# Retention and an MLP on one core: two tiles' 64-row matmuls in one visit, and another order of loads

## The chip, the core and the metric

The kernel runs on one core of a Trainium2 chip. The core has five engines that run side by side, each through its own list of instructions in order: TensorE (PE, matrix products, with its weight loads shown as PEld), VectorE (DVE), ScalarE (ACT), GpSimd (POOL) and SyncE (SP). They wait for one another by semaphores. Data comes by DMA, which an engine issues and which sixteen DMA engines carry out. The metric is the device time of one execution in microseconds (us), as the median of several.

## The reference, cut to what matters

There are 4 batches of 768 positions, 8 heads of 64. First comes a recurrence over positions, then a normalization and a two-layer perceptron with a residual.

```python
gamma = 1.0 - 2.0 ** (-5.0 - np.arange(H))
for t in range(S):
    state = gamma * state + einsum('bhd,bhe->bhde', k[:, :, t], v[:, :, t])
    y[:, :, t] = (1 / sqrt(D)) * einsum('bhd,bhde->bhe', q[:, :, t], state)
x = y.transpose(0, 2, 1, 3).reshape(B, S, 512)
xn = (x - mean(x)) / sqrt(var(x) + 1e-6) * g_ln
out = x + maximum(xn @ w_ch1, 0) @ w_ch2        # 512 x 2048, 2048 x 512
```

## The kernel before

The 768 positions of a batch are cut into 6 chunks of 128. A chunk of one batch is a tile, so there are 24 tiles of 128 rows by 512 columns. Tiles 0 to 3 are the first chunks of the four batches; tiles 4 to 8 are the other chunks of batch 0, tiles 9 to 13 those of batch 1, and so on.

Inside a tile the recurrence becomes matrix products. The tile's keys and queries are needed transposed. For tiles 0 to 7 PE transposes them (L498, L505) and ACT and DVE bring them from PSUM to SBUF, the queries times the decay `qsc` (L510, `eq`). For later tiles SP issues a transposing DMA (L520, `tr`) and DVE multiplies (L527). Then PE makes the scores of the 8 heads (`e_pa`, L538): 8 matmuls whose contraction is 64 rows, a head's width. DVE multiplies them by the decay mask (`e_am`, L562, `am`). The part of the result that comes from earlier chunks is queries times the state: for tiles 0 to 7 in full 128-row matmuls (L582), for tiles from 8 on (`T0`) in 8 matmuls of 64 rows (`e_ps`, L548), which stand right before the scores in most tiles. PE then adds masked scores times values (`e_py`, L572 and L586). The state is built by POOL (`vg`, L633: values times a decay), PE (`e_pd`, L645) and DVE (`e_pb`, L659).

DVE takes the tile's statistics (L601, L602, `bn`), then normalizes (L613, `xn`); ACT keeps a copy for the residual (L619, `xc`). From tile 8 on the result lies in two PSUM banks, even heads in one and odd heads in the other, so these steps work by halves. The normalized tile is transposed by PE (L672, tiles 0 to 7) or by a DMA (L686). The first layer (`e_m1`, L719) works on groups of 1, 2 or 4 tiles (8 groups of one, 4 of two, 2 of four), 16 matmuls of 128 columns, 16 of 256 in two pieces, or 4 of 512 to a piece; ACT, or DVE at L734, applies the relu (L732) into `h1`. The second layer (`e_m2`, L757) takes 16 matmuls of 512 columns to a tile, in four parts; DVE adds the residual (L767) and ACT issues the store (L774). Short idle times early on are filled with matmuls on zeros (L785, `warm`).

PSUM has eight banks: one for the state, two for the first layer, two for the scores, and three (`b0`, `b1`, `b2`) for the rest. Of these the late tiles' result holds `b1` and `b2`, and the second layer goes through `b0`, in the last tiles through all three.

The order of all instructions is fixed by hand: `ORDER` lists the numbers of the tasks in the order in which they are emitted, and each engine gets its own in that order. POOL issues all loads of q, k, v (L430; float32 in HBM, bfloat16 in SBUF) and of the weights in quarters (L438): v0, k1, q1, v1, the first quarter of w1, k2, q2, the second quarter, v2, k3, q3, v3, the third, and so on. The k and q of tile 0 come in halves through SP and ACT (L401). From tile 8 on, one-element copies (L447) hold POOL back until an earlier load has landed.

Of the kernel before, what the change touches and what calls it, by code (L numbers as in the profile page):

```python
# [14 lines left out]
PE, ACT, DVE, POOL, SP = range(5)  # L15

CFG = {
    "T0": 8, "TX": 8, "groups": [1] * 8 + [2] * 4 + [4] * 2,
    "first": ["iota", "pos", "v0", "k1", "q1", "v1", "w1_0", "k2", "q2", "w1_1", "v2",
              "k3", "q3", "v3", "w1_2", "k4", "q4", "v4", "k5", "q5", "v5", "w1_3", "w2_0",  # L20
              "k6", "q6", "v6", "k7", "q7", "v7", "w2_1", "w2_2", "w2_3"],
    "bufs": {"qsb": 6, "ksb": 5, "vsb": 9, "qk": 8, "tr": 6, "vg": 3, "trq": 3, "trk": 3},
    "load_pad": 600, "w_pad": 550, "lead": 32, "lead2": 32, "sq_at": 28000, "late_load": 1700, "two": 4, "m2b": ("b0",), "m2all": 16, "inter": 4, "every": 4, "tail": (0, 384, 512), "step": 8, "pace": 8, "ahead": 3,
    "slack": 600, "tr_pad": 4000, "x_pad": 3500, "vg_pad": 2500, "fill": 0.8, "fill_end": 14000,
}

ORDER = [int(x) for x in """
16 17 2 0 3 19 20 23 14 8 15 1 24 5 7 9 25 4 10 6 13 21 11 26 18 45 22 27 146 28 149  # L30
100147 148 150 46 29 151 30 162 100163 153 12 152 165 154 164 166 155 31 156 157 167 32
158 168 169 47 100176 159 170 524 177 178 160 179 100172 214 180 181 171 173 532 33 215
182 183 525 184 534 161 190 533 193 34 35 36 526 100191 186 535 192 194 10527 187 540 37
38 185 542 195 48 196 49 39 541 216 197 204 40 42 43 41 536 198 50 217 543 207 234
100205 206 528 537 200 52 51 201 544 199 208 10529 224 209 545 552 188 548 10549 553 174
100225 210 227 550 551 546 53 55 175 226 228 211 54 212 44 218 219 547 213 554 530 220
555 251 202 221 235 100241 229 538 230 56 244 10531 236 556 539 242 275 231 558 100258
557 232 559 243 560 10561 237 562 57 245 246 233 238 239 563 222 566 259 564 247 260 567
248 189 261 570 262 252 565 568 249 60 254 255 250 569 223 253 203 263 100722 61 268 58
59 62 287 298 63 723 716 724 301 66 67 64 717 65 264 725 269 718 571 719 265 726 266 270  # L40
720 576 100271 276 307 267 578 272 579 577 728 273 68 69 278 277 72 729 730 731 318 73
279 70 299 71 280 580 572 732 281 300 282 74 322 284 286 734 735 75 288 581 283 285 736
302 303 290 289 573 737 291 738 574 319 584 292 740 741 293 320 294 296 742 308 304 240
585 78 575 743 582 744 295 297 310 333 79 76 309 77 339 586 305 583 311 80 746 587 334
747 312 335 313 314 274 316 323 81 315 748 84 350 749 351 588 592 317 325 85 82 83 379
750 589 256 257 324 354 326 727 602 86 752 87 753 327 328 329 603 593 590 754 755 594
591 330 90 331 340 352 332 342 756 341 343 721 380 598 321 599 595 91 758 336 759 344
760 761 596 733 88 345 89 355 762 346 368 348 353 600 92 757 745 739 337 597 347 93 764
96 349 97 94 381 601 95 765 98 338 357 604 356 766 606 386 99 605 382 607 767 358 306
359 383 614 612 768 360 384 615 361 613 363 770 397 102 771 103 100 362 772 398 365 364  # L50
763 369 101 104 371 370 773 403 610 372 608 774 611 373 776 616 609 399 366 105 374 387
108 109 617 375 618 414 367 377 106 107 777 620 418 751 376 378 389 619 110 388 778 390
779 622 415 391 385 404 780 392 393 621 623 630 782 395 111 114 429 115 631 394 112 400
456 113 433 626 116 624 117 396 406 120 121 416 405 430 783 627 625 407 784 431 408 628
419 409 634 785 410 629 632 411 412 457 118 119 122 413 421 635 786 445 633 420 123 788
126 458 422 127 789 646 124 423 424 790 425 427 647 401 125 426 428 791 642 638 434 436
792 435 794 795 796 639 643 465 769 437 438 640 417 439 440 442 128 797 459 641 129 441
446 443 476 132 644 798 432 402 133 645 636 130 448 447 648 131 134 138 637 460 650 449
450 649 800 651 461 451 452 801 802 477 454 803 444 775 480 462 453 466 478 455 135 491
804 136 137 468 492 467 806 139 495 807 469 470 140 493 808 471 141 809 472 142 474 473  # L60
475 652 653 654 481 483 482 484 810 655 656 658 143 510 479 485 144 787 506 805 657 799
145 659 660 661 486 662 507 496 487 489 664 663 488 508 490 666 498 497 665 499 667 668
670 669 500 671 501 502 672 673 504 511 812 674 503 505 676 513 512 675 514 678 463 677
680 515 679 682 813 681 814 683 516 494 811 509 517 781 519 464 518 520 815 100830 831
816 521 832 818 819 200824 820 825 684 817 793 685 826 690 688 691 827 689 694 696 833
695 522 686 697 687 708 709 821 698 699 692 693 523 822 848 700 828 834 702 100842 701
703 706 707 704 200836 714 837 705 715 712 838 849 843 713 710 711 850 844 845 839 846
851 840 100854 852 855 856 823 847 841 835 829 853 857 860 861 858 862 863 864 859 865
""".split()]


class Plan:

    def __init__(self, seen, begin, first_load):
        self.seen, self.begin, self.first_load = seen, begin, first_load  # L80
        self.tasks, self.bufs, self.chosen = [], {}, {}

    def pool(self, name, n):
        self.bufs[name] = n

    def add(self, eng, ns, rank, emit, after=(), takes=None, uses=(), load=0, hw=0, lat=0, at=0,
            follows=(), slack=0, slots=None):
        after = [d for x in after for d in (x if isinstance(x, list) else [x])]
        t = {"on": eng if isinstance(eng, dict) else {eng: ns}, "rank": rank, "emit": emit,
             "after": after, "takes": takes, "uses": list(uses) + ([takes] if takes else []),  # L90
             "slots": (slots or [(takes[0],)]) if takes else [],
             "load": load, "hw": hw, "lat": lat, "at": at, "follows": list(follows),
             "slack": slack}
        self.tasks.append(t)
        return t

    def order(self, seq):
        left, ends = {}, {}
        for t in self.tasks:
            for u in t["uses"]:  # L100
                left[u] = left.get(u, 0) + 1
        held = {name: [] for name in self.bufs}
        free = dict(self.begin)
        sw_free, hw_free, out = self.first_load, 0, []
        for number in seq:
            t = self.tasks[number % 10000]
            e = sorted(t["on"])[number // 10000 % 10]
            at = max(free[e], sw_free - 7000 if t["load"] else 0)
            for d in t["after"]:
                own = d["eng"] == e and not (d["load"] or d["hw"] or d["lat"] and e != POOL)  # L110
                at = max(at, d["end"] if own else d["seen"])
            got = []
            for options in t["slots"]:
                name = options[number // 100000 if len(options) > 1 else 0]
                got.append(name)
                if len(held[name]) == self.bufs[name]:
                    if left[held[name][0]]:
                        raise RuntimeError("a buffer is taken too early")
                    at = max(at, ends[held[name][0]])
            t["eng"], t["start"], t["ns"] = e, at, t["on"][e]  # L120
            t["end"] = free[e] = at + t["ns"]
            t["seen"] = t["end"] + self.seen[e] + t["lat"]
            if t["load"]:
                sw_free = max(t["end"] + 800, sw_free) + t["load"]
                t["seen"] = sw_free + 700 + t["lat"]
            if t["hw"]:
                begun = max(at + 600, hw_free)
                queued = max(0, sw_free - begun)
                hw_free = begun + t["hw"] + min(queued, 2 * t["hw"])
                if queued:  # L130
                    sw_free += t["hw"] * 2 // 3
                t["end"] = free[e] = max(t["end"], hw_free - 900)
                t["seen"] = hw_free + 1050 + t["lat"]
            for name in got:
                if len(held[name]) == self.bufs[name]:
                    held[name].pop(0)
# [684 lines left out]
```

## Time and profile before

| | us |
|---|---|
| median of 3 runs | 215.06 (215.06 to 215.4) |
| span of the profiled execution, first to last instruction | 212.1 |
| the median beyond that span | 3.0 |
| PE busy in the span | 204.2 |
| DVE busy | 121.6 |
| POOL busy | 95.8 |
| ACT busy | 85.0 |

The profile gives no separate device time for the profiled execution; its span is set beside the median. Busy time counts overlapping matmuls once, and the end of a matmul is modelled, so a busy PE says that work was in it, not that it ran at its peak. The start times of matmuls in the timeline are therefore the surer guide: two 128-column matmuls of a stream start 0.056 us apart, two of 512 columns 0.216. A row of a timeline gives start, duration, engine, line, operation, output and inputs, and how many instructions were merged in it. A row of the windows table gives a stretch and its length, then the busy time and the number of instructions of PE, PEld, DVE, ACT and POOL, the granted clock of PE (1.00 is full), the DMA share and GB/s.

### The profile page before, as it was taken

To read this page: it belongs to the slowest core of one execution; us is meant where nothing else is said; L and a number is where in the kernel's file an instruction comes from. 1 tells how busy PE (TensorE), PEld (TensorE's weight loads), DVE (VectorE), ACT (ScalarE), POOL (GpSimd) and SP (SyncE) were. 2 spreads that over 40 slices of the span, in tenths; PEclk is the share of its full clock that TensorE was granted. 3 is DMA by queue.
4 is the path that set the end of the run, shared out by engine and by line. 5 is a ranking of instruction groups with operands and counts; after the bars stand their busy time and mean duration, and the time that the engine had idled before them with its cause. 6 is when DMAs were issued, how large, how long until landed. Compare 5 with 4: busy or idle time off the path is not lost.

```text
span 212.1 us, 4939 instructions
## 1 busy us (share of the span) xinstructions
PE 204.2 (96%) x2005; PEld 130.8 (62%) x2027; DVE 121.6 (57%) x264; ACT 85.0 (40%) x173; POOL 95.8 (45%) x149
## 2 busy tenths in 40 slices
PE   7988999999999999999999999999999999999993
PEld 3468999975667666657576676574444444444442
DVE  6776778674566875664775777478676510030041
ACT  5485556750431323332352442351366601444200
POOL 8988697238776584657855837430000000000000
PEclk9999999999999999999999999999999999999999
DMA  9999999999999999999999999959440260000035
GB/s 130 174 180 180 163 198 173 208 139 114 112 100 93 155 119 177 168 269 145 134 145 181 105 173 84 157 83 151 86 157 10 65 185 3 0 0 0 0 141 209
DMA packets 108890, 26.85 MB, mean 127 GB/s; under 512 B 101569, under 2 KB 105921, under 8 KB 108866
## 3 DMA queue, kind: packets, MB, share of 16 engines
q0 software_dynamic: 77024, 13.37, 83.7%
q1 hardware_dynamic: 27186, 6.59, 21.1%
q10 hardware_dynamic: 4656, 6.56, 9.0%
q8 instruction: 16, 0.26, 0.5%
q14 instruction: 8, 0.07, 0.1%
HBM read 27.30 MB, written 6.29 MB: 158 GB/s over the span
## 4 chain that ended last, share of the span: by engine, by line
PE 87%; DMA 8%; POOL 3%; issue 1%; DVE 0%; POOLq 0%
PE b L757 39%; PE mm L719 38%; DMA ksb<-in_k_dram 4%; DMA w<-in_moe_w_ch_dram 3%; PE pa L538 2%; PE pd L645 2%; PE b L572 2%; PE b L548 2%; POOL v L430 1%; PE b L498 1%; PE b L672 1%; POOL vg L633 0%; PE b L586 0%; PE b L582 0%; PE b L505 0%
## 5 line engine op out<-in xcount | busy, mean ns | idle before, releaser
L719 PE MATMUL mm<-xnt,w 128*128 128x128 bf16 (+2 forms) x896 | 95.5, 257 | 0.2 <-ACT xnt L256 0.2
L757 PE MATMUL b<-w,h 128*128 128x512 bf16 (+2 forms) x379 | 88.4, 370 | 1.2 <-issue 0.2
L732 ACT ACTIVATE h<-mm 128x512 bf16<-128x512 f32 x91 | 53.8, 599 | 81.4 <-PE mm L719 81.1
L719 PEld LDWEIGHTS <-w 128*128 128x128 bf16 x896 | 66.0, 98 | 20.5 <-issue 0.2
L757 PEld LDWEIGHTS <-h 128*128 128x128 bf16 x400 | 37.1, 98 | 37.7
L562 DVE TENSOR_TENSOR asb<-pa,mask 128x1024 bf16<-128x1024 f32 x24 | 29.4, 1224 | 19.9 <-PE pa L538 19.7
L767 DVE SCALAR_TENSOR_TENSOR osb<-b,rstd,x_all 128x512 f32<-128x512 f32 (+2 forms) x25 | 18.0, 726 | 25.9 <-PE b L757 25.6
L601 DVE BATCH_NORM_STATS2 bns<-b 128x6 f32<-128x256 f32 (+1 forms) x40 | 17.8, 477 | 17.7 <-PE b L572 10.9
L619 ACT CAST x_all<-b 128x256 bf16<-128x256 f32 (+1 forms) x40 | 16.2, 416 | 22.5 <-DVE xn L613 20.3
L613 DVE SCALAR_TENSOR_TENSOR xn<-b,mv,gb 128x256 bf16<-128x256 f32 (+1 forms) x40 | 20.1, 532 | 0.7
L633 POOL TENSOR_TENSOR vg<-vsb,vsc 128x512 bf16<-128x512 bf16 x16 | 16.6, 1044 | 6.7 <-PE pd L645 5.9
L430 POOL DMA_DIRECT2D vsb<-in_v_dram x20 | 18.0, 901 | 2.7 <-issue 1.6
L659 DVE TENSOR_TENSOR state<-pd,gch 64x256 bf16<-64x256 f32 x40 | 16.6, 415 | 4.1 <-PE pd L645 3.2
L430 POOL DMA_DIRECT2D qk<-in_k_dram x16 | 14.3, 892 | 2.6 <-issue 2.0
L430 POOL DMA_DIRECT2D qk<-in_q_dram x16 | 14.2, 890 | 0.7 <-issue 0.7
L447 POOL COPY scrap<-qk 1x1 bf16<-1x1 bf16 x30 | 5.4, 181 | 13.4 <-DMA qk<-in_k_dram 11.7
L447 POOL COPY scrap<-vsb 1x1 bf16<-1x1 bf16 x15 | 2.6, 177 | 16.4 <-DMA vsb<-in_v_dram 16.3
L700 DVE RECIPROCAL rstd<-rstd 128x1 f32<-128x1 f32 (+2 forms) x14 | 2.2, 157 | 12.9 <-ACT rstd L694 12.8
L785 PE MATMUL pd<-zeros 128*128 128x512 bf16 (+1 forms) x24 | 6.6, 420 | 1.3 <-DVE zeros L291 1.2
L438 POOL DMA_DIRECT2D w<-in_moe_w_ch_dram x8 | 6.2, 776 | 3.0 <-DMA w<-in_moe_w_ch_dram 3.0
L572 PEld LDWEIGHTS <-asb 128*128 128x128 bf16 x128 | 5.8, 98 | 2.4
L527 DVE TENSOR_TENSOR trq<-tr,qsc 128x512 bf16<-128x512 bf16 x16 | 6.9, 432 | 0.0
(68 smaller groups left out, 127.9 us busy)
## 6 DMA issues: line engine op xcount, KB each, us to landing
out_dram<-osb ACTq DMA_DIRECT2D x23, 256.0 KB, 3.2
w<-in_moe_w_ch_dram POOLq DMA_DIRECT2D x8, 512.0 KB, 10.0
vsb<-in_v_dram POOLq DMA_DIRECT2D x20, 128.0 KB, 5.4
qk<-in_k_dram POOLq DMA_DIRECT2D x16, 128.0 KB, 4.7
qk<-in_q_dram POOLq DMA_DIRECT2D x16, 128.0 KB, 4.9
qsb<-in_q_dram POOLq DMA_DIRECT2D x7, 128.0 KB, 9.1
v<-in_v_dram POOLq DMA_DIRECT2D x4, 128.0 KB, 7.0
ksb<-in_k_dram POOLq DMA_DIRECT2D x4, 128.0 KB, 9.5
```

Source lines behind the costliest of these rows:

```text
L430: nc.gpsimd.dma_start(out=tile_of(kind, j), in_=src)
L562: nc.vector.tensor_tensor(out=take("asb", t, [P, NPAIR, 2, P], BF16).rearrange("p i a t -> p a i t"), in0=held["pa", t], in1=mask.rearrang ...
L572: nc.tensor.matmul(half_y[h % 2][:, h // 2 * D:(h // 2 + 1) * D], lhsT=held["asb", t][:, h // 2, h % 2, :], rhs=tile_of("v", t)[:, h, :], ...
L601: nc.vector.bn_stats(out=bns[:, t, i, :], in_=x)
L613: nc.vector.scalar_tensor_tensor(out=dst, in0=src, scalar=mv[:, t, 0:1], in1=g, op0=ALU.subtract, op1=ALU.mult)
L619: nc.scalar.copy(out=dst, in_=src)
L633: e.tensor_tensor(out=take("vg", j, [P, H, D], BF16), in0=tile_of("v", j), in1=vsc[:, cc, :].unsqueeze(2).to_broadcast([P, H, D]), op=ALU. ...
L659: nc.vector.tensor_tensor(out=held["pb", n][o, :, o], in0=held["pd", b][o, :, o], in1=gch[o, cc, :].unsqueeze(2).to_broadcast([D, NPAIR, D ...
L719: nc.tensor.matmul(p[:, j, :], lhsT=w1[:, ko, (ho + j) * P:(ho + j + 1) * P], rhs=held["xnt", hb][:, h0:h0 + n, ko, :], start=(ko == 0), s ...
L732: nc.scalar.activation(out=dst, in_=src, func=AF.Relu)
L757: nc.tensor.matmul(held[key][:, 0:w], lhsT=held["h1", hb][:, ho, i * P:(i + 1) * P], rhs=w2[:, ho, cols], start=(ho == 0), stop=(ho == HO ...
L767: nc.vector.scalar_tensor_tensor(out=take("osb", key, [P, w], FP32), in0=held[key][:, 0:w], scalar=rstd[:, t:t + 1], in1=x_all[:, t, cols] ...
```

## The change

The planner, the task numbers and the tile pools go. Each buffer is a fixed tile, used in turn, and the order is a list of names, emitted one after the other. A token such as `m7_8//Ub` says: the first layer of group 7, piece 8, in PSUM bank Ub; `r3_0/D`: its relu on DVE.

The eight PSUM banks are laid out anew: `X` and `U` of two banks each, `Y0`, `Y1`, `M` and `PD`. The scores of a tile take X or U; the first layer's outputs take the same four banks one at a time (`Xa`, `Xb`, `Ua`, `Ub`). The second layer goes through `M`, and near the middle and the end also through `Y0`, `Y1` and `PD`.

From tile 8 on, tiles go in pairs (8, 9), (10, 11) to (22, 23). One `vis` emits on PE the scores of both tiles, one in X and one in U, and then the state parts of both, with nothing between. The results of both tiles share Y0 (even heads) and Y1 (odd heads), each tile in its half of the bank.

```diff
+ 'pairs': [(8, 9), (10, 11), (12, 13), (14, 15), (16, 17), (18, 19), (20, 21), (22, 23)],
+    def y_of(t, par):
+        o = visit[t].index(t) * NPAIR * D
+        return BANK[("Y0", "Y1")[par]][:, o:o + NPAIR * D]
...
+    @on("vis")
+    def _(eng, first):
+        ts = visit[first]
+        for t in ts:
+            for i in range(NPAIR):
+                for par in range(2):
+                    o = slice(D * par, D * (par + 1))
+                    nc.tensor.matmul(pa_of(t)[:, par, i * P:(i + 1) * P], lhsT=kT(t)[o, i, :],
+                                     rhs=slot(trq, t)[o, i, :], start=True, stop=True)
+        for t in ts:
+            for i in range(NPAIR if t >= T0 else 0):
+                for par in range(2):
+                    o = slice(D * par, D * (par + 1))
+                    nc.tensor.matmul(
+                        y_of(t, par)[:, i * D:(i + 1) * D], lhsT=slot(trq, t)[o, i, :],
+                        rhs=slot(state, chunk(t) - 1)[o, i, o], start=(i == 0 and t == ts[0]), stop=False,
+                        skip_group_check=True)
```

There are three state tiles instead of two, and the cast of k0 moves from ACT to DVE. The order begins as follows. `hk0`, `hq0` are the halved loads of tile 0 and `hkc0`, `hqc0` their casts; `k`, `q`, `v` are POOL's loads; `W` and `Z` are quarters of w1 and w2; `g` stands for a one-element copy that holds POOL back (`gq8`, `gk8`), except `gb`, `gl`, `gch`, which make constants; `z` is a part of the second layer.

```diff
+hk0b/A hk0a/S iota pos small lmul consts hq0b/A grow k1 q1 q2 hq0a/S touch vsc v0 cm idn arg
+hkc0/D k3 hqc0b/A qsc hqc0a/D k2 warm12_1 tq0//Y0 warm0_3 tk1//Y1 tk0//M gb//Ub zero mask eq0 k4
+v1 ek1 ek0 gl tq1//Y1 vis0//X eq1 q3 am0 warm1_0 tq2//Y0 q4 v2 eq2 warm3_2 py0//M vis1//U am1
+bn0 tk3//Y0 v3 warm1_2 tk2//Y1 W0 ek3 ek2 W1 warm3_1 vis2//U tk4//Y1 ek4 v4 vg0 xn0 am2 xc0 gch
+py1//Y1 tq3//Y0 eq3 sq0 W3 q5 bn1 vis3//U tq4//Y0 xn1 v5 k5 eq4 xc1 am3 tx0//Y0 pd0 py2//M
+tx1//Y1 ex0 vis4//X ex1 bn2 q8 vg4 k8 py3//Y0 m0_0//Ua xn2 am4 tx2//Y1 m1_0//Ub bn3 pb4 ex2 xc2
+r1_0/A sq2 m2_0//Xb m0_4//Xa r2_0/A q6 W2 r0_0/D xn3 py4//M xc3 m1_4//Ub bn4 tx3//Y1 m2_4//Ua k6
...
+vis8//X,U z2_2 am9 gk12 z2_3 am8 tr12 py9 m7_8//Ub k13 gv11 py8 v12 gq12 vg11 pb11 ad2 rs6 bn8
+bn9 m7_12//Xa m7_4//Xb r7_12/A r7_4/A r7_8/A z3_0//M q13 z3_1 xn9b xn8a xn9a m7_0//Xa xc8a xc9b
```

So POOL loads k1, q1, q2, v0, k3, k2, k4, v1, q3, q4, v2 and v3 ahead of the first quarter of w1 (W0), then W1, v4, W3, q5, v5, k5, q8, k8, q6 and W2. After that, leaving the one-element copies and `vg` out, come k6, v8, q9, v6, k9, q7, k7, q10, Z0, v7, k10, Z1, q11, Z3, k11, v9 and Z2. SP's first transposing DMA of q and k, for tile 11, stands after this, before those of tiles 8, 9 and 10. Between one visit and the next from tile 8 on, PE has parts of the second layer, pieces of the first, the state and the outputs of the two tiles.

## The prediction

> **What bounds the kernel now.** I read the page first, its span and its line of busy engines, then the chain that ended last.
>
> ```profile
> span 212.1 us, 4939 instructions
> ...
> PE 204.2 (96%) x2005; PEld 130.8 (62%) x2027; DVE 121.6 (57%) x264; ACT 85.0 (40%) x173; POOL 95.8 (45%) x149
> ...
> PE 87%; DMA 8%; POOL 3%; issue 1%; DVE 0%; POOLq 0%
> ```
>
> TensorE is the bound. The question is only where it isn't: the windows table answers.
>
> ```profile
> 10.00:13.00 3.00, 2.47 (x25) 1.42 (x26) 2.32 (x3) 2.04 (x3) 2.67 (x5) 1.00 1.91 177
> 13.00:16.00 3.00, 2.60 (x46) 2.27 (x43) 2.37 (x5) 2.66 (x6) 2.67 (x3) 1.00 1.69 184
> 16.00:19.00 3.00, 2.64 (x52) 2.56 (x50) 1.85 (x4) 0.99 (x2) 2.23 (x3) 1.00 2.15 171
> 19.00:22.00 3.00, 2.64 (x50) 2.45 (x48) 2.54 (x6) 2.06 (x5) 2.03 (x3) 1.00 1.70 184
> 22.00:25.00 3.00, 2.63 (x52) 2.51 (x49) 2.61 (x6) 1.99 (x4) 1.97 (x3) 1.00 2.43 155
> 25.00:29.00 4.00, 4.00 (x76) 3.79 (x74) 2.06 (x3) 2.56 (x8) 3.91 (x6) 1.00 1.53 196
> ```
>
> The first number after the stretch is its length, the second PE's busy time: there are holes until about 25 us and none after. So the time is (what PE lost) + (PE's work), and I price both. Work, from start-to-start times in the PE timeline: sixteen 128-column matmuls of L719 0.893, sixteen 256-column ones 1.75, eight 512-column ones 1.73, four 512-column ones of L757 0.865, a group of four transposes or of four state matmuls (L645) 0.223, the eight of L572 or L586 0.235. All of L719 is 28.6 + 28.0 + 27.7, all of L757 83.1, the rest about 28.1 with the switches below: 195.5 us. The last matmul ends near 208.8, so PE lost 13.3 us. By 28.97 us it had done 11 blocks of L719 (9.8), 16 groups of transposes and state (3.6), 5 score groups (5 x 0.405) and 4 of L586 (0.9): 16.4 us of work, 12.6 lost. After that only 0.7 us is lost in 180.
>
> The timeline of one late tile, PE alone in these rows, shows what a visit to the 64-row form costs:
>
> ```profile
> 104.42 0.39 PE L645 MATMUL pd<-vg,qk 128*128 128x128 bf16 x4
> 104.74 0.29 PE L548 MATMUL b<-state,trq 64*128 64x64 bf16 x8
> 104.87 0.39 PE L538 MATMUL pa<-trq,tr 64*128 64x128 bf16 x8
> 105.19 1.04 PE L757 MATMUL b<-w,h 128*128 128x512 bf16 x4
> ```
>
> Four 128-column matmuls take 0.22 elsewhere; here 0.32 pass before L548 starts: 0.095 to enter. The eight of L538 run in pairs, 4 x 0.056 = 0.22, and again 0.32 pass: 0.095 to leave. A visit costs 0.19 beyond its work. The waits view agrees: the weight load of L548 sat idle 3.8 us in 12 waits that nothing in the trace ended.
>
> **The merged visits: -1.9 us.** Before, the 16 late tiles make 18 visits: at 95.48 and 146.17 L548 and L538 are parted by other matmuls. After, `vis` emits the scores and then the state parts of two tiles with nothing between: 8 visits. 10 x 0.19 = 1.9 us, on the chain, since PE has no holes there. The early eight tiles keep their single visits.
>
> **The start: +0.9 us.** POOL's loads land one after another. Landing is issue time plus time to landing in the DMA view: v0 at 6.56, the w1 quarters at 11.8, 16.1, 22.2 and 29.8, w2's first at 32.4. With the loads between them that is 0.87 us for a q, k or v tile and 2.55 for a weight quarter. Now twelve tile loads (k1 to v3) precede W0, so they land from 6.56 to 6.56 + 11 x 0.87 = 16.1, W0 at 18.7 (7 us later than before), W1 21.3, W3 24.7, W2 32.4.
>
> Until W0, PE can do attention alone, and DVE paces that. Start-to-start times on DVE in before's timeline: mask multiply (`am`) 1.13, statistics (`bn`) 1.02, `xn` 0.67, `eq` 0.34, a relu 0.60. The chain: q0 lands at 5.2; ACT casts half and only then makes `qsc`; DVE, which now also casts k0, zeroes three state tiles instead of two (0.8) and makes the mask (1.2) before `eq0`, 7.3; on PE the fp32 `gb` (1.06) stands ahead of visit 0: 8.4, against 6.64 before. So am0 8.9, am1 11.0, bn0 12.1, xn0 13.1, am2 13.8, bn1 15.3, xn1 16.3, am3 17.3, bn2 18.4, xn2 19.5, am4 20.1, bn3 21.2, pb4 22.3, r0_0 22.9, xn3 23.6 to 24.3. PE: m0_0 at 18.75 (W0), tx2 at 20.2 (xn2 ended 20.15, a hole of 0.55), m1_0, m2_0, m0_4 to 23.2, py4 (pb4) to 23.7, m1_4, tx3 24.55, then m2_4, m2_12, pd4, m3_4, tq5, tk5, m0_12 back to back to 29.0. By then PE has done 9 blocks of L719 (8.0), 18 groups (4.0), 5 score groups (2.0), 4 groups of tile outputs (0.9) and py4 (0.46): 15.5, so 13.5 lost, against 12.6. That is +0.9. Bounds: if the three DVE steps ahead of eq0 and `gb` hid wholly the start would gain the 0.55 hole and about 0.6 more, -0.2; if each wait I set to 0.05-0.15 were the 0.3-0.4 that PE's own waits in this stretch show (three of 0.4, two of 0.2-0.3), some five of them in a row add 1.2: +2.1.
>
> What was saved in exchange: tile 4's `xn`, at 31.1 before, now ends near 26. That buys slack, not PE time.
>
> Between 13.7 and 18.5 PE would be busy about a third of the time, and no warm-up matmuls stand there (they end with `warm3_1`, near 12). Before, the granted clock is 1.00 in every window above, with PE never under 80% busy, so its rows can't price this. The nearest row is the cold start: the 512-column warm-ups start 0.427 apart from 1.6 to 4.1 us, those after 5.8 us 0.216. A half clock from 18.75 for as long as that, some 3 us, would cost 1.5. No drop is seen after the start, so I take 0 and keep 1.5 within the high end.
>
> [...] No row of before shows a drop after the start. [...]
>
> **w2 just in time: +0.2 us.** w2 moved from the 28-44 us stretch to behind 32 tile loads. By the same sum its third quarter, Z2, lands at 6.56 + 31 x 0.87 + 8 x 2.55 = 53.9. PE's work ahead of its first user, z0_2: 28 blocks (25.0), four L757 pieces (3.5), 30 groups (6.7), 8 score groups (3.2), eight tile outputs (2.8): 41.1 + 13.5 lost = 54.6. SP's transposes for tiles 8 to 11 start with tr11, at k11's landing near 51, so one is in flight beside Z2. Before, v9 beside a transpose took 5.3 us to land (46.72 to 52.05) where k9 alone took 3.4. Z2 thus lands between 53.9 and 55.8: a wait of 0 to 1.2; I take half the delay, 0.2. If PE is late at the start, this wait shrinks by as much: the two don't add in full.
>
> **The tight pairs: 0 (0 to +1.0).** A visit fills all four banks X and U, which the L719 outputs now share, and writes Y0 and Y1 for two tiles, so the next visit waits for both tiles' last `xn` and `xc`. Window between visits 8-10, 10-12, 14-16, 16-18, 20-22: six L757 pieces (5.2), four L719 blocks (3.5), outputs and state (0.7), the visit 0.7: about 10.2 us. DVE in it: two each of am, bn, eq, four xn (0.40), two pb, about 1.5 add (0.67): 8.8 us, ending in the last `xn` near 9.0 and its copy at 9.4, ahead of the next visit by some 0.7. PE has L757 pieces to do while the two am (2.3) free X and U. So it fits, barely. If each of the five windows slips by 0.2: +1.0. The 0.7 us that before lost in the middle I let stand as the same size.
>
> **What hides for free.** Two more relus go to DVE, which is idle for 43% of the span; static buffers issue nothing; the end (last add, last store on ACT's queue behind st22) has the same instructions. If the new order made st22 delay the last store, the store's 3.2 us landing bounds it; I see 23 before 22's there as before, 0.
>
> **Sum.** -1.9 + 0.9 + 0.2 + 0 = -0.8 on the span of 212.1, so 211.3. The median 215.06 lies 3.0 above the profiled span and I carry that over: **214.3 us**.
>
> **Rivals.**
> 1. *The start is no dearer* (0.25): DVE's chain for tiles 0 to 4 is quicker than my walk and PE fills with m blocks from 18.7 without holes. For it: every load lands before DVE wants it. Against: eq0 stands behind three DVE steps and a late `qsc`. Gain 1.9, with 0.1 for Z2: 213.3.
> 2. *The gain is eaten in the middle* (0.18): Z2 at 55.8 costs 1.0 more and the tight pairs some of theirs, or the merged visits save less than 0.19 each, which is the case where the change doesn't do what it says. Gain about 0: 215.1.
> 3. *Slower: W0 behind twelve loads starves PE* (0.22). Place: 13 to 24 us. PE holds nothing but attention, each hole there is lost for good, and if the clock falls or DVE's chain slips, saturation comes late. Price: the 1.5 of a half clock atop 0.9, or the +2.1 bound, with 0.3 to 0.6 of the tight pairs and Z2: +2.7 against -1.9, 215.9. It decides from a start loss of 1.9 us, that is when PE becomes hole-free after about 25.5 us or m0_0 starts after about 19.7.
>
> The forecast itself gets 0.35. **Chances.** A difference of 0.2% (0.43 us) is about what can be told from no change. Faster: rival 1 (0.25) and nine tenths of the forecast (0.32): 0.57. Same: a tenth of the forecast and most of rival 2: 0.18. Slower: rival 3 and a piece of rival 2: 0.25. **Range** 213.0 to 216.2: from rival 1 with the low bound of the start to rival 3 without its worst.
>
> **What would show it.** Right: 8 visits, no 0.095 steps inside one; lost PE time by 29 us near 13.5; first L719 near 18.8; xn3 ending near 24.3; z0_2 waiting little on w2 near 54.6; PE hole-free windows from 60 us. Wrong: granted clock under 1.00 between 14 and 22 us, waits of L757 on w2 over 1 us, waits of the visits on `xn` or `x_all`, transposed tiles 8 and 9 landing after 60 us.

## The result and the profile after

The changed kernel takes **238.95 us** (median of 4 runs, 238.84 to 239.71), the kernel before 215.06 beside it: a ratio of 1.111, 95% interval 1.106 to 1.116. It is 23.9 us slower; the forecast was 214.3, its range ended at 216.2. The page of the changed kernel, with the lines that answer to those of before (span, busy engines, chain of work by engine):

```profile
span 237.1 us, 4956 instructions
...
PE 209.7 (88%) x2031; PEld 134.3 (57%) x2031; DVE 128.6 (54%) x285; ACT 70.1 (30%) x153; POOL 96.3 (41%) x149
...
PE 59%; DVE 21%; DMA 8%; ACT 6%; issue 3%; ACTq 1%; SPq 0%; DVEq 0%
```

DVE, 0% of the chain before, is 21% of it now. ACT lost 15 us of work and DVE gained 7: something moved between them that the prediction had not counted. The same windows as before, and one later (length, busy PE, PEld, DVE, ACT, POOL, then the granted clock):

```profile
13.00:16.00 3.00, 1.22 (x24) 0.95 (x24) 2.14 (x6) 0.00 (x0) 3.00 (x4) 1.00 2.13 163
16.00:19.00 3.00, 0.86 (x15) 0.60 (x13) 2.93 (x6) 2.64 (x8) 3.00 (x5) 0.90 1.23 207
19.00:22.00 3.00, 2.43 (x30) 2.04 (x30) 2.44 (x6) 0.59 (x1) 0.67 (x1) 0.50 1.58 192
22.00:25.00 3.00, 3.00 (x34) 3.00 (x35) 2.93 (x5) 0.59 (x1) 2.20 (x3) 0.50 1.72 183
25.00:29.00 4.00, 3.12 (x57) 3.00 (x56) 2.99 (x7) 1.02 (x3) 2.25 (x3) 0.97 2.43 159
...
40.00:50.00 10.00, 7.50 (x127) 6.88 (x125) 7.81 (x15) 2.71 (x7) 7.05 (x11) 1.00 1.53 187
```

The third window (19 to 22 us) looks busy only because its clock is half. And the holes don't end at 25 us, as they did before: between 40 and 50 us a quarter of PE's time is idle. What PE waits for in the whole run (total, times, longest), the first lines of the waits view:

```profile
PE X L508 <- ACT h L519: 8.7, 11, 1.8
PE X L508 <- DMA xnt<-xn: 2.9, 3, 1.5
PE X L395 <- DVE trk L246: 2.8, 3, 1.3
PE X L508 <- DVE h L521: 2.6, 4, 1.0
```

L508 is the first layer and L519 and L521 its relus on ACT and DVE, L395 the scores, L246 a PSUM copy on DVE. In before the first layer waited 0.2 us for anything.

To place the loss, I subtract from the time that has passed the work that PE has done, each matmul at the start-to-start time that the prediction used (191.4 us for the whole kernel, the same for all kernels here within 0.2; steps into and out of the 64-row form, and warm matmuls, count as lost). Most traces lack some matmul records, so a value is good to about half a microsecond. "A" and the other letters name the causes below.

| PE time lost by | 30 us | 60 us | 130 us | the end |
|---|---|---|---|---|
| before | 12.5 | 13.5 | 15.5 | 17.2 |
| after | 18.8 | 26.2 | 32.6 | 42.1 |
| after, copies on ACT (A undone) | 16.9 | 23.4 | 30.6 | 37.5 |
| after, one bank to a tile (B undone) | 19.1 | 20.9 | 26.5 | 30.5 |
| after, both | 15.5 | 18.5 | 26.1 | 29.4 |
| base (e9: all mends, reordered) | 14.1 | 14.6 | 20.4 | 21.4 |
| base with A put back | 19.5 | 21.4 | 25.0 | 27.3 |
| base with B put back | 15.1 | 20.5 | 28.1 | 36.2 |
| last version (e17) | 14.2 | 14.6 | 18.0 | 19.0 |

**Cause A, in the code and the trace.** The tokens `ek0` to `ek7` and `ex0` to `ex7` carry no engine letter, and the helper that they call sends everything that isn't "A" to DVE. So the sixteen copies of transposed keys and normalized tiles changed engine. Groups of before, then of after:

```profile
L256 ACT COPY xnt<-b 128x512 bf16<-128x512 bf16 x8 | 4.7, 587 | 5.1 <-PE b L672 5.1
L256 ACT COPY trk<-b 128x512 bf16<-128x512 bf16 x8 | 4.6, 581 | 2.0 <-PE b L498 2.0
```

```profile
L246 DVE COPY trk<-Y 128x512 bf16<-128x512 bf16 x6 | 2.4, 413 | 0.8 <-PE Y L372 0.8
L246 DVE COPY xnt<-Y 128x512 bf16<-128x512 bf16 x5 | 2.1, 422 | 1.7 <-PE Y L482 1.7
L246 DVE COPY xnt<-M 128x512 bf16<-128x512 bf16 x3 | 1.2, 415 | 0.2 <-PE M L482 0.2
L246 DVE COPY trk<-M 128x512 bf16<-128x512 bf16 x2 | 0.8, 416 | 1.6 <-PE M L372 1.6
```

6 + 5 + 3 + 2 are the sixteen. One is shorter on DVE than on ACT (0.41 against 0.58 us), which is beside the point: they stand in the queue of the engine that paces the start.

**Cause B.** X and U are each one tile of two banks, and the order of writes and reads is kept for a tile, not for a bank. A relu of bank Ua therefore waits for the last matmul emitted before it into Ub, and a block for Ua for the relu of Ub. In the compiled program 23 first-layer matmuls wait for a relu of the other bank, and 23 relus for a matmul into the other bank. A hole of 1.3 us in the timelines of PE and then ACT:

```profile
110.14 1.04 PE L508 MATMUL X<-xnt,w 128*128 128x256 bf16 x8
111.02 1.03 PE L531 MATMUL Y<-w,h 128*128 128x512 bf16 x4
111.88 1.04 PE L508 MATMUL X<-xnt,w 128*128 128x256 bf16 x8
114.09 1.14 PE L508 MATMUL X<-xnt,w 128*128 128x256 bf16 x9 [1.17 <-ACT h L519]
```

```profile
112.95 0.60 ACT L519 ACTIVATE h<-X 128x512 bf16<-128x512 f32 x1 [4.88 <-PE X L508]
113.45 0.59 ACT L519 ACTIVATE h<-X 128x512 bf16<-128x512 f32 x1
```

The blocks are `m9_2` (Xa), `m9_6` (Ua) and, after the hole, `m10_6` (Xa). ACT had been idle for 4.88 us. Its next relu, `r9_4`, reads Ub, whose block ended at 103.8 (the last third of a row of 24 matmuls at 101.03, not shown); it starts at 112.95, when `m9_6` into the other half of U ends, and that is the matmul that it waits for in the compiled program. The relu of Xa is queued behind it, and `m10_6` waits for that one. (The page gives both tiles the name X.) Before, the first layer's outputs went through two buffers of one bank each, so that no bank waited for another.

**Cause D.** The one-element copies on POOL wait for an earlier load to land, and every later load stands behind them. POOL's waits in after, then in before:

```profile
POOL scrap L366 <- DMA v<-in_v_dram: 22.5, 8, 5.3
POOL scrap L366 <- DMA qk<-in_k_dram: 16.2, 9, 4.8
POOL scrap L366 <- DMA qk<-in_q_dram: 11.8, 6, 6.0
```

```profile
POOL scrap L447 <- DMA vsb<-in_v_dram: 16.3, 9, 3.5
POOL scrap L447 <- DMA qk<-in_k_dram: 11.7, 5, 6.5
```

50.5 us are held back now, 29.3 before (1.3 of them for q, in a line not shown).

### The profile page after: what moved, and what is told of

Read it like the earlier page. It is cut to its first block, busy times and chain, and to the rows that moved or that the text cites. A ratio compares the mean times of both kernels' runs of the same rounds, so it can differ in the third digit from the quotient of the medians.

```text
span 237.1 us, 4956 instructions
## 1 busy us (share of the span) xinstructions
PE 209.7 (88%) x2031; PEld 134.3 (57%) x2031; DVE 128.6 (54%) x285; ACT 70.1 (30%) x153; POOL 96.3 (41%) x149
## 4 chain that ended last, share of the span: by engine, by line
PE 59%; DVE 21%; DMA 8%; ACT 6%; issue 3%; ACTq 1%; SPq 0%; DVEq 0%
PE X L508 28%; PE M L531 11%; PE Y L531 7%; DMA xnt<-xn 7%; PE PD L531 5%; ACT h L519 5%; DVE xn L442 4%; DVE bns L432 4%; DVE asb L408 3%; DVE state L471 2%; PE X L395 2%; DVE osb L538 2%; DMA osb<-in_q_dram 2%; DVE trq L386 2%; DVE h L521 1%
## 5 line engine op out<-in xcount | busy, mean ns | idle before, releaser
L508 PE MATMUL X<-xnt,w 128*128 128x128 bf16 (+2 forms) x896 | 95.2, 259 | 15.2 <-ACT h L519 8.7
L508 PEld LDWEIGHTS <-w 128*128 128x128 bf16 x896 | 67.5, 99 | 38.7 <-issue 17.5
L519 ACT ACTIVATE h<-X 128x512 bf16<-128x512 f32 x88 | 50.1, 600 | 118.1 <-PE X L508 109.1
L531 PE MATMUL M<-w,h 128*128 128x512 bf16 (+1 forms) x240 | 54.7, 369 | 0.0
L408 DVE TENSOR_TENSOR asb<-X,mask 128x1024 bf16<-128x1024 f32 x24 | 28.6, 1217 | 7.8 <-PE X L395 7.6
L453 POOL TENSOR_TENSOR vg<-v,vsc 128x512 bf16<-128x512 bf16 x20 | 21.1, 1059 | 12.0 <-DMA v<-in_v_dram 9.0
L471 DVE TENSOR_TENSOR state<-PD,gch 64x256 bf16<-64x256 f32 x40 | 16.7, 416 | 13.4 <-PE PD L461 13.0
L531 PE MATMUL Y<-w,h 128*128 128x512 bf16 x96 | 23.2, 379 | 0.0
L337 POOL DMA_DIRECT2D v<-in_v_dram x24 | 21.6, 905 | 2.0 <-issue 1.7
L442 DVE SCALAR_TENSOR_TENSOR xn<-Y,mv,gb 128x256 bf16<-128x256 f32 (+1 forms) x36 | 17.1, 505 | 2.5 <-PE Y L424 1.2
L432 DVE BATCH_NORM_STATS2 bns<-Y 128x6 f32<-128x256 f32 (+1 forms) x36 | 14.6, 442 | 6.6 <-PE Y L424 6.6
L337 POOL DMA_DIRECT2D qk<-in_q_dram x16 | 14.6, 910 | 0.9 <-issue 0.8
L337 POOL DMA_DIRECT2D qk<-in_k_dram x16 | 14.4, 902 | 1.2 <-issue 1.1
L531 PE MATMUL PD<-w,h 128*128 128x512 bf16 (+1 forms) x64 | 14.4, 366 | 0.0
```

The costliest lines, as they stand in the source:

```text
L337: nc.gpsimd.dma_start(out=dst, in_=tok[kind][TILES[t]])
L408: nc.vector.tensor_tensor(out=slot(asb, t).rearrange("p i a t -> p a i t"), in0=pa_of(t).rearrange("p a (i t) -> p a i t", t=P), in1=mask. ...
L432: nc.vector.bn_stats(out=bns[:, t, i, :], in_=x)
L442: nc.vector.scalar_tensor_tensor(out=dst, in0=src, scalar=mv[:, t, 0:1], in1=g, op0=ALU.subtract, op1=ALU.mult)
L453: nc.gpsimd.tensor_tensor(out=slot(vgs, chunk(t)), in0=v_of(t), in1=vsc[:, c, :].unsqueeze(2).to_broadcast([P, H, D]), op=ALU.mult)
L471: nc.vector.tensor_tensor(out=slot(state, chunk(t) - 1)[o, :, o], in0=pd[o, :, o], in1=gch[o, c - 1, :].unsqueeze(2).to_broadcast([D, NPAI ...
```

## The experiments

Seventeen kernels ran. The first eight ran once each beside one run of before (214.1 or 215.0 us); the others were timed in rounds, and their ratios to before carry intervals. Between those, a difference of ratios of 0.01 is 2.1 us. The twelve runs of e17 lie between 215.6 and 218.3 us, so a difference of less than some 3 us between two single runs shows little.

**A and B, alone and together.** e1 adds the letter to sixteen tokens of the changed kernel; e2 gives each bank its own tile, and the mask multiply then goes in two halves; e3 is both.

```diff
-v1 ek1 ek0 gl tq1//Y1 vis0//X eq1 ...
+v1 ek1/A ek0/A gl tq1//Y1 vis0//X eq1 ...
```

```diff
-    X = [ps.tile([P, 2, 4 * P], FP32, name=f"X{i}") for i in range(2)]
-    BANK = {"Xa": X[0][:, 0], "Xb": X[0][:, 1], "Ua": X[1][:, 0], "Ub": X[1][:, 1]}
-    for name in ("Y0", "Y1", "M", "PD"):
+    BANK = {}
+    for name in ("Xa", "Xb", "Ua", "Ub", "Y0", "Y1", "M", "PD"):
```

> The changed kernel with its 16 PSUM copies of tiles 0 to 7 (transposed keys and normalized tiles) given back to ACT. In the changed trace they run on DVE (0.41 each, x8 and x8), and PE waits for them by name. Theory A (the copies make DVE the pacing engine of the first 60 us, and DVE's backlog holds PE): the holes in PE before 60 us fall from about 14.5 us to under 7, the time from 238.9 to 226-231. Theory B (the waits come from two-bank PSUM tiles: an access to one bank waits for the other bank's): holes after 60 us stay, and many before stay too, 235-239. Theory C (PE's clock, granted at 0.74 between 20 and 30 us, is the start's loss): little change while the clock still falls, 236-239.

Measured 234.15: 4.8 less. A is a cause, smaller than expected.

> The changed kernel with X and U cut into four tiles of one bank each; the mask multiply of a tile then goes in two halves of 512 columns, which costs DVE some 0.15 us more to a tile. Theory A: the first 60 us stay as they are, 235-240. Theory B: PE's waits on a relu (8.7 us in 11 waits, and 2.6 from the relus on DVE) go, and the holes after 60 us fall from about 14 us to under 7: 228-233.

Measured 227.14: 11.8 less, a little more than expected. B is the largest.

> Both edits: copies on ACT and one bank to a tile. If A and B together are the cause and my count of the start was right otherwise, PE loses about what the prediction summed and the time is 214-219; each of them alone being the whole cause would give the same time as that edit alone. Theory C, if the clock still falls at about 19 us: 3 us more, 217-222.

Measured 226.13. The two don't add (4.8 + 11.8 would be 16.6, 12.8 came), and 12 us stay open: the expectation missed, there are more causes.

**C, the clock.** e4 adds 19 wide matmuls on zeros to the changed kernel between 11 and 18 us.

```diff
-... W1 warm3_1 vis2//U ...
-py1//Y1 tq3//Y0 ... bn1 vis3//U ... am3 tx0//Y0 pd0 py2//M
+... W1 warm8_1 vis2//U ...
+warm2_1 py1//Y1 tq3//Y0 ... bn1 warm7_0 vis3//U ... am3 warm5_0 tx0//Y0 pd0 py2//M
```

> The changed kernel with 19 more 512-column matmuls on zeros in front of the four places between 12 and 19 us where PE stood idle for 0.7 to 1.7 us. They take the idle time alone, if their number is right. Theory C: the granted clock stays 1.00 and the time falls by half of the 7 us at half clock, to 235-236. Theory A or B: the holes that follow grow by what the clock gives, 237-239.

Measured 239.52. The clock was mended and the time was not. Windows of e4, 10 to 30 us:

```profile
10.00:20.00 10.00, 9.53 (x97) 5.40 (x97) 8.50 (x16) 3.23 (x9) 9.78 (x12) 1.00 2.03 175
20.00:30.00 10.00, 7.42 (x142) 6.94 (x139) 8.47 (x17) 2.94 (x6) 5.00 (x7) 1.00 1.95 173
```

The clock is 1.00 in both; PE, faster, simply waits 2.6 us of the second window. It lost 18.2 us by 30 against 18.8, and by 60 us 25.6 against 26.2: DVE's chain sets when the next work is there. So the fall of the clock at 18.4 us isn't what after loses. The end time alone would not say so: e4's clock fell once later, from 99.1 to 102.5 us, and a half clock of 3.4 us can, by estimate, cost up to 1.7. e5 asks the same on e3.

```diff
-py1//Y1 tq3//Y0 ... bn1 vis3//U ... am3 tx0//Y0 pd0 py2//M
+warm3_0 py1//Y1 tq3//Y0 ... bn1 warm5_0 vis3//U ... am3 warm5_0 tx0//Y0 pd0 py2//M
```

> The version with both edits (copies on ACT, one bank to a tile; 226.1) and 13 more 512-column matmuls on zeros in front of the three places between 13 and 18 us where PE idled for 0.8 to 1.1 us. Its clock falls at 15.8 and is back at 23, 7 us at half. Theory C: the clock stays full, PE's loss by 30 us falls from 15.5 to 12.5 or less and the time to 222.5-224. If the start's loss is passed on to later waits (loads, transposes) and not to the end: 225-226.5.

Measured 226.72, no gain on 226.13: of the 1.3 us won by 30 us (14.2 lost against 15.5) about 0.5 were left by 100 us, before any other fall of the clock in either run.

**E and D: w2's order, and the gates.** e6 is e3 with two load tokens exchanged, e7 is e3 without the 45 one-element copies, e8 is e3 with e5, e6 and e7 together.

```diff
-m5_12//Ub bn6 q11 m5_0//Ua r5_12/A xn6 m5_8//Ub rs0 eq7 Z3 ...
+m5_12//Ub bn6 q11 m5_0//Ua r5_12/A xn6 m5_8//Ub rs0 eq7 Z2 ...
...
-... r5_8/A z1_0//Y0 am7 Z2
+... r5_8/A z1_0//Y0 am7 Z3
```

> The version with both edits, with the third and fourth quarters of w2 loaded in the order in which PE wants them. PE waited 2.0 us for the third at 57 us. If loads set that point, the wait goes and 1.5-2 us with it: 224-224.6. If what comes after (late transposes) sets the end, nothing: 225.8-226.4.

Measured 222.53: in e3 a second-layer piece waited 1.9 us for w2 near 57 us, and that went. It is 3.6 us less, below both ranges; the 1.7 us beyond that wait are not explained, and are within the spread of single runs.

```diff
-m0_12//Ua ek5/A gq8 v8 vis5//X ... ex4/A gk8 q9 ...
+m0_12//Ua ek5/A  v8 vis5//X ... ex4/A  q9 ...
```

> The version with both edits, without the 45 one-element copies that hold POOL back until a load has landed; buffers alone hold it then. Theory D (after 60 us the loads of q, k, v come too late because POOL waits some 50 us on these copies, so their transposes and the visits behind them are late): the holes after 60 us, some 10 us, fall by half or more, 219-222. Rival: the copies keep loads from crowding the transposes, and without them the transposes land later: 226-232.

Measured 218.96: 7.2 less, the low end of theory D's range.

> The three edits together on top of both: if their gains add (3, 1.8 and 5), 215-218; if the copies' removal hurts, 222-230.

Measured 219.67: the gains don't add, and no range had this number. With the gates gone w2's order and the warm matmuls show no gain (218.96 without them), and two holes of 1.4 and 2.3 us stayed, at 74 and 123 us, each a first-layer block that waits for a DMA transpose of normalized tiles (cause **F**).

**F, the late transposes.** e9 is e8 with the order changed near those two places; it is the base of what follows.

```diff
-r7_0/A ex9  v13 z3_2 eq11 xn8b sq8 xc8b xc9a ex8 ...
+r7_0/A ex9  xn8b ex8 v13 z3_2 eq11 sq8 xc8b xc9a ...
...
-m10_6//Xa m8_12//Ub ad7 eq15 ... r9_14/A m9_10//Ub z6_3 m10_4//Xb ... m9_12//Xa
+m8_12//Ub ad7 eq15 ... r9_14/A m9_12//Xa m9_10//Ub r9_12/A z6_3 m10_6//Xa m10_4//Xb ...
```

> The version with all four mends (copies on ScalarE, one bank per tile, w2's third quarter before the fourth, no gate copies, more warm matmuls) still lost 5.8 us more of TensorE's time than before. This kernel only reorders it further: tile 8's second xn half stands ahead of eq11, the transposes of normalized tiles 9 and 8 are issued before tile 13's load, two L531 pieces go ahead of the first first-layer block of tiles 8 and 9, and the first block of tiles 12 and 13 goes behind three blocks and two L531 pieces that do not read them. Theory F (the two remaining holes of 1.44 and 2.34 us are waits for transposes issued too late, and the clock of 0.83 after the second follows from it): both holes go, 3.5 to 4.5 us, so 215 to 216. Rival (those holes only hide another wait, of the second layer or of the visits, that comes next): 218 to 219.5.

Measured 218.34, ratio 1.022 (1.017 to 1.026): the rival's number. Three holes, of 1.6, 1.1 and 1.9 us, at other blocks; the first is no late transpose but a second-layer piece that waits for its bank. Two further orders went after them: e13 puts the output of tile 4 earlier on DVE and more blocks ahead of late transposes, e17 puts the normalizations of tiles 8 to 11 together.

```diff
-... m8_0//Xa py10 py11 pb12 bn11 m8_4//Ua ... r8_0/A ad4 ex10
+... m8_0//Xa py10 py11 pb12 ad4 bn11 m8_4//Ua ... r8_0/A ex10
...
-am17 py16 m11_6//Xa bn16 ... xn16b z10_2 r11_2/A q21 st7/A z10_3 ...
+am17 py16 z10_2 z10_3 m11_6//Xa bn16 ... xn16b r11_2/A q21 st7/A ...
```

> The reordered mended version (218.3 at the last run) kept three holes on TensorE after 60 us: 1.6 at 79.8 us, where a second-layer piece waits for bank M behind four VectorE steps; 1.1 at 85.8 and 1.9 at 124.3, where a first-layer block waits for the transpose of normalized tiles. Here the output of tile 4 stands ahead of the statistics of tiles 10 and 11 on VectorE, two blocks of tiles 8 and 9 go ahead of the first of tiles 10 and 11, and two second-layer pieces ahead of the first block of tiles 14 and 15. Theory F: 3 to 4.5 us go, so 214 to 215.5, about level with the kernel before, with only the start (1.6 us dearer) against the merged visits. Rival (the holes move on to the next tile pair): 217 to 218.5.

Measured 216.32, ratio 1.009 (1.006 to 1.012): between the two.

```diff
-... xn9b xn8a xn9a m7_0//Xa xc8a xc9b r7_0/A ex9  xn8b ex8 ...
+... xn9b xn9a ex9 xn8a xn8b ex8 m7_0//Xa xc9b xc9a r7_0/A ...
...
-am17 py16 z10_2 z10_3 m11_6//Xa ...
+am17 py16 m10_8//Xa r10_8/A z10_2 z10_3 m11_6//Xb r11_6/A ...
```

> The last version (216.3, ratio 1.009 to before) kept four holes after 70 us (0.78 at 76.0, 0.57 at 82.8, 0.87 at 125.8, 0.85 at 129.6) and the dearer start (14.3 lost by 30 us against 12.5). Here VectorE's normalizations of tiles 8 to 11 stand together ahead of everything else and their transposes are issued at once, one first-layer block of tiles 12 and 13 moves behind the ninth visit pair as cover for tiles 14 and 15, and the relus of that group are issued in the order in which their blocks end. Theory F with the sum of the forecast (start 1.6 to 1.8 dearer, merged visits 1.6 to 1.9 cheaper, nothing else): 213.8 to 215, level with before. Rival (each hole closed opens the next, since TensorE arrives earlier at the same late transposes): 215.8 to 217.

Measured 216.02, ratio 1.0076 (1.0043 to 1.0109). That is the rival's number again, and its interval overlaps e13's. After 20 us one hole over 0.5 us is left (1.0, at 128 us). From e9 to e17 the new order won 1.4%; how much of it was transposes and how much the waits for a bank, no run separates. The last version is still 0.8% slower than before.

**One cause put back at a time**, on e9. First B, with the diff of e2 reversed:

> The first kernel of this call with only X and U made two-bank tiles again, as in the changed kernel, with the mask multiply in one instruction. Theory B (waits are kept per tile, so a relu of one bank waits for the last matmul written into the other, and the next first-layer block for the relu of the other): with every other cause mended the time still rises by 5 to 11 us, the loss lying in the stretches where first-layer blocks follow one another (30 to 60 and 100 to 130 us). Rival (in the changed kernel the two-bank tiles hurt only since VectorE and the transposes were late as well): within 2 us.

Ratio 1.083 (1.078 to 1.087) against 1.022: **13 us**, beyond the expected range. The table shows where: 1.0 us by 30 us, 4.9 between 30 and 60, 1.8 between 60 and 130 and 7.1 after that, so the end counts for more than the stretches that the expectation named. Its waits of PE begin as in after:

```profile
PE X L508 <- ACT h L519: 9.0, 12, 1.8
PE X L508 <- DVE h L521: 2.9, 4, 1.0
```

> The reordered mended version (218.3) with the sixteen copies of transposed tiles put back on VectorE, as in the changed kernel. Theory A (VectorE paces the first 60 us, so 16 copies of 0.41 us are a loss of TensorE's time of some 3 to 6 us, as when they were moved in the changed kernel, 4.8): 221 to 224. Rival (between the two-bank kernels with and without them the gain was 4.8 and with one bank per tile only 1.0, so they cost only where relus hold the banks): 218.5 to 219.7.

(The diff of e1 reversed.) Ratio 1.040 (1.034 to 1.046): 4 us, and by 30 us PE had lost 19.5 us against 14.1 (up to 1.6 of it, by estimate, by a half clock from 26.5 us on). Theory A holds, with the middle of its range. (e14 to e16 were timed in other rounds than e9, each beside before.)

> The reordered mended version (218.3) with the 45 one-element copies on GpSimd put back, each before the load that it stood before. Theory D (each waits for an earlier load to land and holds back all later loads on its queue, so tiles from 11 on come late): 223 to 226, the loss after 60 us. Rival (the reordering has given enough slack): 218 to 219.5.

(The diff of e7 reversed.) Ratio 1.030 (1.025 to 1.035): 1.7 us, with intervals that overlap a little. In e9, without these copies, POOL waits 43.8 us at `vg` for loads of v instead. In e3 the same copies cost 7.2; how much they cost depends on the slack of the order around them. Neither theory had this number.

> The reordered mended version (218.3) with w2's fourth quarter loaded ahead of its third again, as in the changed kernel. Theory E (the third quarter is wanted by the third second-layer piece at about 55 us and lands 2 to 3 us too late): 220 to 222.5, a wait of the second layer on w2 in the trace. Rival (without the gate copies the loads run far enough ahead): 218 to 218.8.

(The diff of e6 reversed.) Ratio 1.013 (1.009 to 1.018), not above e9's: theory E falls here, the rival holds. That it came out 0.9% below e9, which nothing explains, shows how far two such ratios can be off: A's 1.9% is clear of that, the gates' 0.8% is not.

**The start, and the price of a visit.** e10 is e9 with w1's first quarter two loads earlier and tile 0's first block taken forward.

```diff
-... tq2//Y0 q4 v2 eq2 ... warm1_2 tk2//Y1 W0 ek3/A ...
+... tq2//Y0 q4 W0 v2 eq2 ... warm1_2 tk2//Y1 ek3/A ...
...
-... am3 warm5_0 tx0//Y0 pd0 py2//M tx1//Y1 ex0/A vis4//X ...
+... am3 warm3_0 m0_0//Xa r0_0/A pd0 py2//M tx1//Y1 vis4//X ...
```

> On top of the former: w1's first quarter is loaded two tile loads earlier, tile 0's normalized transpose goes to bank M right after its xn, and its first first-layer block runs at about 17.5 instead of 19.5 us in place of warm matmuls, with its relu on ScalarE. Theory S (the order of the start, with w1 behind twelve loads, costs about 1.5 us against the kernel before, which nothing later gives back): TensorE's loss by 30 us falls from 14.0 to about 12.9 and the time by about 1 us against the former kernel. Rival (VectorE's chain for tiles 0 to 4 paces the start and not w1): no gain, within 0.3 us.

Ratio 1.025 (1.021 to 1.028): no gain. The first block ran at 17.7 instead of 19.4 us, but the second at 21.3 instead of 20.6, and by 30 us PE had lost 14.4, not 14.1. The block taken forward delayed `py2` (18.8 against 17.9), with it DVE, and the second block's transpose then waited 0.9 us for DVE's `xn`. In e9 the first block waited 0.3 us for w1, and DVE worked from 11.0 to 24.4 us without a pause of note. It isn't w1 that paces the start, it is DVE.

e11 is e9 with the visits parted: the visit emits one tile, and a token for the other tile stands behind the next piece of PE work.

```diff
-vis8//X,U z2_2 am9  z2_3 am8 ...
+vis8//X,U z2_2 vis9 am9  z2_3 am8 ...
...
-... vis12//X,U z5_2 am12 ...
+... vis12//X,U z5_2 vis13 am12 ...
```

> The first kernel of this call with the eight pair visits parted again: other matmuls (second-layer pieces or a group of state matmuls) stand between the scores and state parts of one tile and those of its neighbour, nothing else is changed. Theory V (each visit to the 64-row form costs 0.19 us of TensorE's time, as before's timeline shows): eight more visits cost 1.5 us, so the time rises by 1.2 to 1.7. Rival (the steps around a visit are hidden or belong to something else): within 0.3 us, in which case the change did not hold the gain that its merging seemed to bring.

Ratio 1.031 (1.025 to 1.036) against 1.022: 1.9 us more, with intervals that overlap a little. The timeline is firmer. First the merged visit in the changed kernel, then two parted ones in e11:

```profile
83.43 0.62 PE L395 MATMUL X<-trq,tr 64*128 64x128 bf16 x16
83.89 0.40 PE L401 MATMUL Y<-state,trq 64*128 64x64 bf16 x16
84.22 0.40 PE L461 MATMUL PD<-vg,qk 128*128 128x128 bf16 x4
```

```profile
84.89 0.28 PE L403 MATMUL Y<-state,trq 64*128 64x64 bf16 x8
85.11 1.04 PE L534 MATMUL M<-w,h 128*128 128x512 bf16 x4
86.08 0.23 PE L397 MATMUL Ua<-trq,tr 64*128 64x128 bf16 x1
...
86.31 0.28 PE L403 MATMUL Y<-state,trq 64*128 64x64 bf16 x8
86.52 1.04 PE L534 MATMUL M<-w,h 128*128 128x512 bf16 x4
```

Merged, two tiles take 0.79 us (83.43 to 84.22). Parted, they take 0.45 (84.66, its first row, to 85.11) and 0.44 (86.08 to 86.52), 0.10 more; and the four matmuls of L534 at 85.11 should let the next start at 85.11 + 4 x 0.216 = 85.97, it starts at 86.08. That is 0.21 for one more visit, 1.7 for eight.

## Why the prediction was wrong

Taken in its own order:

- **Merged visits, -1.9: the price held.** 8 visits, steps inside none, 0.21 to a visit where 0.19 was said. It is the one thing that the change gained. Its condition, that PE has no holes there, did not hold in after.
- **The loads: held but for the last.** W0, W1, W3 and W2 landed at 18.4, 21.9, 25.2 and 33.1 us (18.7, 21.3, 24.7 and 32.4 said). Z2 landed at 57.5, not 53.9: the sum of tile loads left out POOL's waits at the gates. In after that cost nothing, since PE was later still.
- **The start, +0.9: failed, +6.3** (18.8 lost by 30 us against 12.5). The first block came at 22.3 instead of 18.8, `xn3` ended at 28.1 instead of 24.3. The walk through DVE's chain had a row for each step but the copies: eight of the sixteen stand ahead of `xn3`. The rest of the walk was right: in e9, with the copies on ACT, `xn1` starts at 16.27 (16.3 said), `am4` at 20.07 (20.1), and `xn3` runs from 23.67 to 24.42 (23.6 to 24.3). `xn3` in the timelines of DVE, in after and then in e9:

```profile
27.35 0.75 DVE L442 SCALAR_TENSOR_TENSOR xn<-Y,mv,gb 128x512 bf16<-128x512 f32 x1
```

```profile
23.67 0.75 DVE L442 SCALAR_TENSOR_TENSOR xn<-Y,mv,gb 128x512 bf16<-128x512 f32 x1
```

"Two more relus go to DVE" stood under what hides for free, and it is three (8 against 5); the sentence should have been a count of every operation whose engine changes. The code would have shown it, since those tokens have no letter. Of the 6.3 us A took 1.9 (16.9 lost in e1), B, with A undone, another 1.4 (15.5 in e3) and the missing warm matmuls 1.3 (14.2 in e5). The last 1.7 stay in every mended version (14.1 to 14.4 lost) and are more than the 0.9, though within its bounds of -0.2 to +2.1.
- **The tight pairs, 0 (0 to +1.0): the step that failed most.** The price was sought in DVE's time between two visits. The cost was in the first layer, where banks of one tile wait for each other: 13 us on the mended base. It lay before me in the diff (the prediction says that a visit "fills all four banks X and U, which the L719 outputs now share") and was costed at nothing. It also holds at the end, which the prediction called the same: after lost 3.6 us between 200 and 220, the base with one bank to a tile 0.
- **The clock, 0: wrong in the trace, without effect on the end.** It was 0.50 from about 18.4 to 25.2 us (0.90 over 16 to 19 is 0.6 us at half clock, 0.97 over 25 to 29 is 0.24), yet e4 took it away, and by 60 us PE had lost 25.6 us instead of 26.2.
- **w2 just in time, +0.2:** no wait in after. In e3, with A and B mended, it was 1.9 us, the wait that rival 2 named and put at 1.2.
- **Rival 3** (slower, 215.9) had the sign and its signs came: the first block after 19.7, the clock down, DVE's chain late. Its heading did not: W0 landed at 18.4, and w1 behind twelve loads starves nobody (e10); with the copies on ACT the first block came at 19.4. Its price, 2.7 on the start and the pairs, is far from what they cost.

Where the 23.9 us are, from the runs: B 13 and A 4 (each put back on e9), gates 1.7 (the same, not clear of the doubt), the order with its late transposes 3 (e9 to e17), and 1.6 that the last version still lacks: 23.3. It is a sum of steps on one path, not of independent parts, and that it comes near 23.9 proves nothing: in other settings A gave 1.0 to 4.8 and the gates 7.2. What e17 still lacks agrees with its start, 1.7 dearer by 30 us; from there to the end it loses 4.8 where before lost 4.7. So the 1.9 of the merged visits (ten fewer) must have gone into other waits of the tight order; which, no run shows. Whether another order would keep it stays open.

The granted clock was half in after from 18.42 to 25.25 us. From 16 to 18.42 us PE had been busy for 0.86 of 2.42 us, with no hole longer, by start times, than 1.67 us (15.96 to 17.63); while the clock was half, PE was busy for 5.68 of 6.83 us. In e3 it was half from 15.8 us to near 23. In e4 PE was busy for 9.53 of the 10 us from 10 to 20, and the clock stayed 1.00 there and to 30 us. The 0 of the prediction rested on before alone, which has no drop after the start; the windows read from it have PE busy for 82% at least, and so couldn't show what a stretch like that of after does. What makes the clock fall, these runs don't show.

## What to carry to other kernels

When a rewrite changes how engines are chosen, count each engine's operations in the new order by hand, defaults included, before costing anything as moved. When buffers are merged, ask what the unit of waiting is: here two banks in one tile made readers and writers of either bank wait for both, and the price (13 us, e12 against e9) was paid by the first layer, which alternates between them, not by the step that wanted them joined. A gain of 0.2 us a time is safe only while the order around it keeps the slack that the old one had; price the slack that the change spends along with the steps that it saves.

## What was not expected of the hardware

- The clock halved at 18.42 us in after, though no hole in PE's work ahead of that was longer than 1.67 us: from 16 to 18.42 us PE was busy for 0.86 of 2.42 us. It stayed half until 25.25 us, with PE busy for 5.68 of those 6.83 us.
- A transposing DMA of a normalized tile took 2.4 us from issue to landing at its quickest (80.38 to 82.79 in e9) and 6.4 to 6.5 (118.29 to 124.69, 119.58 to 126.11) where four loads of q, k and v and a store were issued between 116.2 and 119.1. That these were the reason is likely, not shown.
- A copy that is quicker on DVE (0.41 us) than on ACT (0.58) was dearer there: sixteen of them cost the whole 4 us (e14 against e9).
